# Merging the split products of a block-diagonal matmul, and moving one small sum by half a step

## The chip, the cores and the metric

The kernel runs on one core of a Trainium2 chip. The engines are named as the profile names them: PE multiplies matrices (PEld is its loading of the stationary operand), DVE works on vectors, ACT evaluates functions and copies, POOL is a second, slower vector engine, and SP issues DMAs. The metric is the device time of one execution in microseconds (us). The kernel before took 314.25 us as the median of three runs (313.38 to 314.42).

## The reference

The input x has 2048 tokens of 640 values, and there are 32 heads of 20 values. Two attention branches work on the same x, and a gate per token mixes them: `out = g*a + (1-g)*b`.

Branch A, which the change touches, is linear attention with a learned feature map:

```
q, k, v = split(x @ wqkv)
phi(t) = [softmax(t @ w_phi), softmax(-(t @ w_phi))]      per head, 20 + 20 features
kv = sum over tokens of phi(k)^T v ;  z = sum over tokens of phi(k)
a = ( phi(q) kv ) / ( phi(q) z + 1e-6 ) @ wo
```

Branch B is causal softmax attention within four segments of 512 tokens, plus a memory that is carried from segment to segment, and its own output matrix.

## The kernel before

The work runs in stages, each with an order written out by hand for every engine. Each engine executes its own list in order, and semaphores join the lists.

**Weight folds.** `t @ w_phi` is linear, so the kernel multiplies `w_phi` into the key and query parts of `wqkv` once (`emit_foldM`, L186). The folded matrix has five row chunks of 128. For the keys the five folds lie at the very start (L317), between transposes of the weights and of x, with ACT copying each result out of PSUM. For the queries they lie in one run (L348) after the key stage.

**Key stage** (L338, until about 53 us). 16 chunks of 128 tokens are projected on keys and values, exponentiated by ACT, normalised by DVE and POOL. After it come the kv sums (L382) and the query projections with their exponentials (`emit_pq`, L416), until about 89 us.

**Numerator stage** (L663, about 89 to 127 us). There are 16 chunks `ch` of 128 tokens, and for each chunk two halves, one for each sign `sgn` of the feature map: 32 halves in all. In a half,

- PE computes a numerator (`emit_num`, L477) of 128 x 640 values into one of three PSUM tiles in turn, three halves ahead of its use, and beside it one half of a projection for branch B (`emit_next_half`, L637: five products of 320 columns, which ACT copies out of one of two PSUM buffers);
- DVE multiplies the numerator by its per-head factor (`emit_tt`, L529) into a tile `tt`, of which there are two, one per chunk;
- after both halves POOL adds the two signs into `oA` (L691), which SP sends through a transposing DMA.

The factors come in batches of four chunks. While batch n is being worked on, the denominators of batch n+1 are computed: PE puts them in the free columns of the numerators of the second chunk (k = 1); DVE takes a reciprocal and a product (`emit_rr`, L505) after each of the two halves of k = 1; DVE then sums both signs (`emit_dsum`, L510) after the first half of k = 2; at the end of k = 2, after POOL's `oA`, DVE takes the reciprocal of that sum (L694) and POOL makes the factors from it in two steps (`emit_cs`, L519: L522 and L524). The next batch's first `emit_tt` waits for these. There are three such turns.

**Heads over chunks.** A head has 20 features, a chunk of features has 128 rows, and a PSUM bank holds 16 heads (320 columns). So a head at the border of two chunks (heads 6, 12, 19 and 25) gets its sum from two products. `PIECES` (L63) lists the products of one numerator or fold as (chunk of 128 features, bank, first head, end head). In the kernel before each border head is a product of its own, with 20 columns, apart from the heads of the same chunk that are complete in it:

```python
PIECES = [(0, 0, 0, 7), (1, 0, 6, 7), (1, 0, 7, 13), (2, 0, 12, 13), (2, 0, 13, 16),
          (2, 1, 16, 20), (3, 1, 19, 20), (3, 1, 20, 26), (4, 1, 25, 26), (4, 1, 26, 32)]
FIRST, LAST = {0, 5}, {4, 9}
```

`FIRST` are the products that open a sum in their bank. A later product of the bank adds where the sum has already written, and writes where it has not. In the kernel before no product does both.

**Branch B** (L1052, about 127 us to the end) is driven by 16 double steps, each with bursts of scores on PE (L770), exponentials on ACT (L774), masks on POOL (L781) and products with the values (L824), with dense products put between them.

Of the kernel before, what the change touches and what calls it, by code (L numbers as in the profile page):

```python
# [15 lines left out]
def kernel(  # L16
# [43 lines left out]


    TH = [(P * j // DH, (P * j + P - 1) // DH + 1) for j in range(KC)]
    PIECES = [(0, 0, 0, 7), (1, 0, 6, 7), (1, 0, 7, 13), (2, 0, 12, 13), (2, 0, 13, 16),  # L63
              (2, 1, 16, 20), (3, 1, 19, 20), (3, 1, 20, 26), (4, 1, 25, 26), (4, 1, 26, 32)]
    FIRST, LAST = {0, 5}, {4, 9}
    HW = 8

    gS = res.tile([P, NCH], F32, name="gS")
# [31 lines left out]
    for what in "c w1 w3 x0 x1 g v0 v1".split():  # L100
        n = int(what[1:]) if len(what) > 1 else 0
# [74 lines left out]
    def w2tile(name):  # L176
        return aps.tile([P, 2, 512], F32, name=name, tag="w2")
# [8 lines left out]
    def emit_foldM(WT, dst, ic, eng=nc.scalar.copy):  # L186
        ps = w2tile("fold_ps")
        for n, (j, bk, lo, hi) in enumerate(PIECES):
            h0 = TH[j][0]
            nc.tensor.matmul(ps[:, bk, (lo - 16 * bk) * DH:(hi - 16 * bk) * DH],  # L190
                             lhsT=WT[:, j, ic * P:(ic + 1) * P],
                             rhs=Wphi[:, j, lo - h0:hi - h0, :].rearrange("p h d -> p (h d)"),
                             start=(n in FIRST), stop=(n in LAST))
        eng(out=dst[:, ic, :].rearrange("p (b n) -> p b n", b=2), in_=ps[:, :, 0:320])

    def emit_xT(n):
# [120 lines left out]
    for step in "P T0a T2d M0a T1d M2a T4d T3d M1a X0 M4a X1 M3a k0 g k1 v0 v1 r0 r1".split():  # L317
        n = int(step[1:2] or 0)
        if step[0] == "T":
            emit_foldT(wnat_k, WkT, n, {"a": nc.scalar.copy, "d": nc.vector.tensor_copy}[step[2]])  # L320
        elif step[0] == "M":
            emit_foldM(WkT, WkA, n, {"a": nc.scalar.copy, "d": nc.vector.tensor_copy}[step[2]])
        elif step[0] == "X":
            emit_xT(n)
        elif step[0] == "P":
            for j in (0, 2):
                emit_Wphi(j, nc.vector)
        elif step[0] == "k":
            emit_a1_mm(n, pks, WkA, 320)
        elif step[0] == "v":  # L330
            emit_a1_mm(n, pvs, WvA, 321)
        elif step[0] == "r":
            emit_a1(n)
            emit_zmove(n)
        else:
            emit_gw()
# [11 lines left out]
    for n in range(KC):  # L348
        emit_foldM(WkT, WqA, n)
# [127 lines left out]
    def emit_num(ch, sgn):  # L477
        qb, qc = divmod(ch, HB // P)
        t = nps[(2 * ch + sgn) % 3].tile([P, 2, 512], F32, name="num")
        for n, (j, bk, lo, hi) in enumerate(PIECES):  # L480
            h0 = TH[j][0]
            nc.tensor.matmul(t[:, bk, (lo - 16 * bk) * DH:(hi - 16 * bk) * DH],  # L482
                             lhsT=Eqs[qb, j][:, sgn, qc * P:(qc + 1) * P],
                             rhs=kvn[:, sgn, j, lo - h0:hi - h0, :].rearrange("p h e -> p (h e)"),
                             start=(n in FIRST), stop=(n in LAST))
        return t

    def num_view(t):
        return t[:, :, 0:320].rearrange("p b (h e) -> p b h e", e=DH)

    def den_view(t):

        return t[:, :, 320:448].rearrange("p n (s h e) -> p n s h e", s=2, e=2)
# [11 lines left out]
    def emit_rr(rr, uu, t, o, n):  # L505
        k = slice(o, o + n)
        nc.vector.reciprocal(out=rr[:, k], in_=t[:, :, :, :, 1])  # L507
        nc.vector.tensor_tensor(out=uu[:, k], in0=t[:, :, :, :, 0], in1=rr[:, k], op=ALU.mult)

    def emit_dsum(uu, n):  # L510
        dd = a3w.tile([P, NB, H], F32, name="dd", bufs=1)
        nc.vector.scalar_tensor_tensor(out=dd[:, 0:n], in0=uu[:, 0:n, 0, :], scalar=1e-6,
                                       in1=uu[:, 0:n, 1, :], op0=ALU.add, op1=ALU.add)
        return dd

    def rr_tiles():
        return (a3w.tile([P, NB, 2, H], F32, name="rr"), a3w.tile([P, NB, 2, H], F32, name="uu", bufs=1))

    def emit_cs(chs, rr, dd, o=0):  # L519
        n = len(chs)  # L520
        k = slice(o, o + n)
        nc.gpsimd.tensor_tensor(out=dd[:, k], in0=dd[:, k],  # L522
                                in1=gS[:, chs[0]:chs[0] + n, None].to_broadcast([P, n, H]), op=ALU.mult)
        nc.gpsimd.tensor_tensor(out=rr[:, k], in0=rr[:, k],  # L524
                                in1=dd[:, k, None, :].to_broadcast([P, n, 2, H]), op=ALU.mult)
        for i, ch in enumerate(chs):
            cs_of[ch] = rr[:, o + i]

    def emit_tt(tt, sgn, ps, cs):  # L529
        csb = cs[:, sgn].rearrange("p (b h) -> p b h", b=2)[:, :, :, None].to_broadcast([P, 2, 16, DH])  # L530
        nc.vector.tensor_tensor(out=tt[:, sgn].rearrange("p (b h) d -> p b h d", b=2),  # L531
                                in0=ps, in1=csb, op=ALU.mult)
# [74 lines left out]
    def slot(ch):  # L607

        return ch + (ch >= EARLY)
# [15 lines left out]
    def emit_turn(part, sc, dst):  # L625
        c = sc % 4
        nc.sync.dma_start_transpose(out=dst[:, :, c * P:(c + 1) * P],
                                    in_=stages[part][sc % 2].rearrange("p h e -> p (h e)"))
# [8 lines left out]
    def emit_next_half():  # L637
        if halves:
            emit_half(pps, *halves.pop(0), nc.scalar.copy)
# [10 lines left out]
    def emit_num_at(i):  # L650
        if i < len(order):
            ch, sgn = order[i]
            t = nums[ch, sgn] = emit_num(ch, sgn)
            if ch % 4 == 1 and ch < NCH - 4:
                for n in range(2):
                    emit_den(den_view(t)[:, n], ch + 3 + 2 * sgn + n)
# [6 lines left out]
    for ch in range(NCH):  # L663
        bt = next(n for n, chs in enumerate(BATCH) if ch in chs)
        k = ch - BATCH[bt][0]
        ahead = BATCH[bt + 1] if bt < len(BATCH) - 1 else None
        tt = a3w.tile([P, 2, H, DH], F32, name="tt")
        for sgn in range(2):
            t = nums.pop((ch, sgn))
            emit_tt(tt, sgn, num_view(t), cs_of[ch])  # L670
            if ahead and sgn == 0 and k == 1:
                rr_n, uu = rr_tiles()
            if ahead and (k, sgn) in ((1, 0), (1, 1)):
                emit_rr(rr_n, uu, den_view(t), 2 * sgn, 2)
            for _ in range((ch, sgn) not in IDLE):
                emit_next_half()
            emit_num_at(2 * ch + sgn + 3)
            if ch - 1 in KEYS and sgn == 0:
                nc.scalar.activation(out=ek, in_=ek, func=ACT.Exp, scale=-1.0)
            elif ch - 1 in KEYS:  # L680
                nc.scalar.activation(out=phik, in_=key, func=ACT.Relu)
            if (ch, sgn) in EXPS:
                part = EXPS[ch, sgn]
                nc.scalar.activation(out=(phiks[1][:, 0] if part == "k" else phiq_st)[:, :, 0:DH],
                                     in_=stages[part][0][:, :, 0:DH], func=ACT.Exp)
            if (ch, sgn) in TWICE:
                emit_next_half()
            if ahead and k == 2 and sgn == 0:
                dd = emit_dsum(uu, NB)
        oA = a3w.tile([P, D], BF16, name="oA", bufs=4)  # L690
        nc.gpsimd.tensor_tensor(out=oA.rearrange("p (h d) -> p h d", d=DH),  # L691
                                in0=tt[:, 0], in1=tt[:, 1], op=ALU.add)
        if ahead and k == 2:
            nc.vector.reciprocal(out=dd, in_=dd)  # L694
            emit_cs(ahead, rr_n, dd)
        while turns_due:
            part, c = turns_due.pop(0)
            emit_turn(part, c, (kTs if part == "k" else qTs)[c // 4])
        nc.sync.dma_start_transpose(out=oTA[:, slot(ch)], in_=oA)
        if ch - 2 in KEYS:  # L700
            nc.gpsimd.tensor_tensor(out=phik, in0=phik, in1=ek, op=ALU.add)
        if ch in KEYS:
            key = stages["k"][KEYS[ch] % 2][:, :, 0:DH]
            phik = phiks[0][:, KEYS[ch], :, 0:DH]
            ek = a3w.tile([P, H, DH], BF16, name="ek")
            nc.scalar.activation(out=ek, in_=key, func=ACT.Relu, scale=-1.0)
# [5 lines left out]
    with ExitStack() as bctx:  # L712
# [487 lines left out]
        for ps, lo in quarters:  # L1200
            for k5 in range(KC):
                nc.tensor.matmul(ps, lhsT=oT4[:, 2, k5, :], rhs=WoB[:, k5, lo:lo + 160],
                                 start=(k5 == 0), stop=(k5 == KC - 1))
# [36 lines left out]
```

## Time and profile before

| what | us |
|---|---|
| median of three runs | 314.25 |
| the profiled execution: its own time | 314.52 |
| its span, from first to last instruction | 312.8 |
| PE busy | 302.4 |
| ACT busy | 251.9 |
| DVE busy | 230.3 |
| POOL busy | 205.6 |
| the 32 numerators (L482): products | 320 |
| the ten folds (L190): products | 100 |
| start of the numerator stage, start of branch B's scores | 88.97, 126.8 |

The profile shows one execution. Busy times are sums over a whole engine, and a busy PE is not the same as PE being the limit: matmuls are pipelined, so a row's duration is longer than the pace at which products follow each other. What limits a stage has to be read from the chain of work (which event released which), taken stage by stage.

### The profile page before, as it was taken

Reading aid. Unit: us, or ns where it says so; the run is one execution under the profiler, and the core shown is the slowest. Engines: PE = TensorE matmul, PEld = TensorE weight load, DVE = VectorE, ACT = ScalarE, POOL = GpSimd, SP = SyncE. Lnnn points to the kernel's source line nnn. Section 1 sums busy time; section 2 is a strip of 40 time slices with the busy share of each in tenths; the row PEclk is TensorE's granted clock in tenths of the full one; section 3 lists DMA queues with packets and bytes.
Section 4 is the critical chain, followed back from the end, with each engine's and each line's share of the span. In section 5 each row is a group of like instructions: output and inputs, shape, how many; then the busy total and the mean of one; then the engine's idle time right before and its main releaser. Section 6 shows DMA issues by size and latency. Waiting matters only on the chain.

```text
span 312.8 us, 9844 instructions
## 1 busy us (share of the span) xinstructions
PE 302.4 (97%) x4038; PEld 205.3 (66%) x4038; DVE 230.3 (74%) x532; ACT 251.9 (81%) x320; POOL 205.6 (66%) x310
## 2 busy tenths in 40 slices
PE   8999999999999999999999999999999999999995
PEld 7788877855578788465656666666666666544573
DVE  3477997998779997767758588788656746667773
ACT  4677888357956549899999899999998999899953
POOL 8588599103346989965666667688886767756560
PEclk9999999999999999999999999999999999999999
DMA  7989934439217998775331358343855556334142
GB/s 223 202 173 188 234 103 127 130 88 365 76 27 99 129 142 132 153 103 105 37 69 36 69 111 121 57 91 61 110 92 90 53 106 116 82 82 97 40 115 84
DMA packets 97414, 35.33 MB, mean 113 GB/s; under 512 B 85722, under 2 KB 97370, under 8 KB 97370
## 3 DMA queue, kind: packets, MB, share of 16 engines
q1 hardware_dynamic: 96794, 34.06, 56.3%
q10 hardware_dynamic: 576, 0.66, 0.7%
q8 instruction: 31, 0.51, 0.7%
q14 instruction: 13, 0.11, 0.1%
HBM read 6.10 MB, written 2.62 MB: 28 GB/s over the span
## 4 chain that ended last, share of the span: by engine, by line
PE 68%; ACT 21%; DVE 5%; POOL 3%; issue 2%; ACTq 0%; DVEq 0%; POOLq 0%
ACT PT L774 18%; PE proj L1008 10%; PE st_ps L770 9%; PE proj L948 8%; PE pq L421 7%; PE pk L240 7%; PE pv L240 7%; PE nda L824 5%; PE proj L561 3%; DVE tt L531 2%; PE num L482 2%; PE kv_ps L394 2%; DVE rr L507 2%; POOL oA L691 1%; PE warm L316 1%
## 5 line engine op out<-in xcount | busy, mean ns | idle before, releaser
L774 ACT ACTIVATE PT<-st_ps 128x1024 bf16<-128x1024 f32 x160 | 153.9, 1024 | 11.3 <-PE st_ps L770 8.9
L781 POOL TENSOR_SCALAR_AFFINE_SELECT PT<-PT 128x512 bf16<-128x512 bf16 (+1 forms) x130 | 83.8, 663 | 42.7 <-ACT PT L774 42.3
L259 POOL TENSOR_TENSOR EkSn<-Ek,krec 128x1280 bf16<-128x1280 bf16 x15 | 35.1, 2358 | 9.2 <-DVE krec L258 7.3
L824 PEld LDWEIGHTS <-PT 128*128 128x128 bf16 x1040 | 32.9, 96 | 7.8 <-issue 4.5
L1008 PEld LDWEIGHTS <-xTf 128*128 128x128 bf16 x300 | 26.5, 97 | 14.1 <-issue 5.5
L824 PE MATMUL nda<-vB,PT 128*128 128x21 bf16 x1000 | 34.2, 173 | 0.0
L1014 DVE CAST Z<-proj 128x320 bf16<-128x320 f32 x44 | 21.2, 489 | 16.4 <-PE proj L1008 15.3
L428 ACT ACTIVATE Eq<-pq 128x1024 bf16<-128x1024 f32 x20 | 19.4, 1021 | 12.6 <-PE pq L421 12.6
L255 DVE TENSOR_REDUCE ksum<-Ek 128x64 f32<-128x1280 bf16 x16 | 23.6, 1475 | 7.2 <-ACT Ek L251 7.2
L948 PE MATMUL proj<-WkA,oTA 128*128 128x320 bf16 x160 | 28.3, 300 | 0.0
L531 DVE TENSOR_TENSOR tt<-num,rr 128x640 f32<-128x640 f32 x32 | 25.0, 813 | 4.4 <-POOL rr L524 1.7
L770 PE MATMUL st_ps<-Z 32*128 32x512 bf16 (+3 forms) x256 | 25.2, 299 | 3.0 <-ACT PT L774 2.5
L691 POOL TENSOR_TENSOR oA<-tt 128x640 bf16<-128x640 f32 x16 | 24.6, 1546 | 5.2 <-DVE tt L531 5.0
L770 PE MATMUL st_ps<-Eq 32*128 32x384 bf16 (+3 forms) x256 | 25.6, 298 | 1.9 <-ACT PT L774 1.5
L251 ACT ACTIVATE Ek<-pk 128x640 bf16<-128x640 f32 x32 | 20.8, 703 | 8.1 <-PE pk L240 7.0
L240 PEld LDWEIGHTS <-xTf 128*128 128x128 bf16 x200 | 22.6, 113 | 4.7
L421 PE MATMUL pq<-xTf,WqA 128*128 128x512 bf16 x100 | 22.4, 379 | 0.3 <-issue 0.3
L948 PE MATMUL proj<-WvA,oT 128*128 128x320 bf16 x120 | 21.2, 300 | 0.0
L948 PEld LDWEIGHTS <-oTA 128*128 128x128 bf16 x160 | 13.5, 97 | 8.6 <-issue 4.6
L561 PEld LDWEIGHTS <-xTf 128*128 128x128 bf16 x180 | 15.8, 97 | 4.6
L770 PEld LDWEIGHTS <-Z 32*128 32x128 bf16 x256 | 7.5, 91 | 16.2 <-issue 15.0
L482 PEld LDWEIGHTS <-Eq 128*128 128x128 bf16 x320 | 15.9, 96 | 3.3 <-issue 0.7
(194 smaller groups left out, 584.8 us busy)
## 6 DMA issues: line engine op xcount, KB each, us to landing
Z<-EkSn SPq DMA_DIRECT2D x32, 160.0 KB, 2.8
out_dram<-orow SPq DMA_DIRECT2D x8, 160.0 KB, 1.8
out_dram<-oTA SPq DMA_DIRECT2D x6, 160.0 KB, 1.8
WvA<-in_A_wqkv_dram SPq DMA_DIRECT2D x2, 400.0 KB, 5.9
WvB<-in_B_wv_dram SPq DMA_DIRECT2D x1, 800.0 KB, 4.6
WkB<-in_B_wk_dram SPq DMA_DIRECT2D x1, 800.0 KB, 6.4
WqB<-in_B_wq_dram SPq DMA_DIRECT2D x1, 800.0 KB, 8.1
WkA<-in_A_wo_dram SPq DMA_DIRECT2D x1, 800.0 KB, 11.2
```

The source lines that it names most:

```text
L240: nc.tensor.matmul(ps[:, bk, 0:n], lhsT=key_tokens(c, sc), rhs=rhs, start=(c == 0), stop=(c == by_row[-1][0] if sc == 0 and W is WkA else ...
L259: (nc.vector if sc == NCH - 1 else nc.gpsimd).tensor_tensor(out=EkSn[:, sc].rearrange("p s (h f) -> p (s h) f", f=DH), in0=Ek.rearrange("p ...
L421: nc.tensor.matmul(pq[:, half, :], lhsT=WqA[:, c, j * P:(j + 1) * P], rhs=xq[:, 2 * qb + half, c], start=(c == 0), stop=(c == KC - 1))
L531: nc.vector.tensor_tensor(out=tt[:, sgn].rearrange("p (b h) d -> p b h d", b=2), in0=ps, in1=csb, op=ALU.mult)
L561: nc.tensor.matmul(ps, lhsT=xq[:, sc // 4, cc, sc % 4 * P:(sc % 4 + 1) * P], rhs=W[:, cc, half * 320:(half + 1) * 320], start=(cc == 0), s ...
L691: nc.gpsimd.tensor_tensor(out=oA.rearrange("p (h d) -> p h d", d=DH), in0=tt[:, 0], in1=tt[:, 1], op=ALU.add)
L770: nc.tensor.matmul(ps[:, i - i0, o:o + L - c * P], lhsT=kT[32 * i:32 * i + 32, c * P:(c + 1) * P], rhs=qT[32 * i:32 * i + 32, c * P:L], st ...
L774: nc.scalar.activation(out=PT[:, i0:i0 + 2], in_=ps, func=ACT.Exp, scale=SCALE_B)
L781: nc.gpsimd.affine_select(out=v, in_=v, pattern=[[0, n_i], [1, P]], compare_op=ALU.is_ge, fill=0.0, base=0, channel_multiplier=-1)
L824: nc.tensor.matmul(nd[:, j, i], lhsT=block(st, c)[:, i, (j - c) * P:(j - c + 1) * P], rhs=vB[:, c, 4 * st.g + i, :], start=(c == 0), stop= ...
L948: nc.tensor.matmul(ps, lhsT=oT[:, k % KC], rhs=W[:, k % KC, hs], start=(k == 0), stop=(k == n - 1))
L1008: nc.tensor.matmul(ps, lhsT=xq[:, sc // 4, k, sc % 4 * P:(sc % 4 + 1) * P], rhs=W[:, k, half * 320:(half + 1) * 320], start=(k == 0), stop ...
```

## The change

The change has two parts.

First, `PIECES` is cut from ten products to six: each is now everything that one chunk of features gives to one bank. Where a chunk holds the rest of a border head and also new heads, one product now adds in its first 20 columns and writes in the others. Both `emit_num` and `emit_foldM` use the list, so 32 numerators and 10 folds lose four products and four weight loads each, 168 in all. The number of columns computed stays 720 per numerator or fold. (`skip_group_check` concerns only the building of the program.)

Second, `emit_dsum` moves from the end of the first half of k = 2 to the end of its second half. On DVE the order is before: tt(k=2, first), dsum, tt(k=2, second), reciprocal; and after: tt(k=2, first), tt(k=2, second), dsum, reciprocal. Nothing else changes place on any engine.

```diff
-    PIECES = [(0, 0, 0, 7), (1, 0, 6, 7), (1, 0, 7, 13), (2, 0, 12, 13), (2, 0, 13, 16),
-              (2, 1, 16, 20), (3, 1, 19, 20), (3, 1, 20, 26), (4, 1, 25, 26), (4, 1, 26, 32)]
-    FIRST, LAST = {0, 5}, {4, 9}
+    PIECES = [(0, 0, 0, 7), (1, 0, 6, 13), (2, 0, 12, 16), (2, 1, 16, 20), (3, 1, 19, 26), (4, 1, 25, 32)]
+    FIRST, LAST = {0, 3}, {2, 5}
...
@@ emit_foldM and emit_num
-                             start=(n in FIRST), stop=(n in LAST))
+                             start=(n in FIRST), stop=(n in LAST),
+                             skip_group_check=True)
...
-            if ahead and k == 2 and sgn == 0:
+            if ahead and (k, sgn) == (2, 1):
                 dd = emit_dsum(uu, NB)
```

More of the change, by code (lines that the diff above doesn't have):

```diff
@@ L484, in emit_num @@
                              rhs=kvn[:, sgn, j, lo - h0:hi - h0, :].rearrange("p h e -> p (h e)"),
-                             start=(n in FIRST), stop=(n in LAST))
+                             start=(n in FIRST), stop=(n in LAST),
+                             skip_group_check=True)
         return t
```

## The prediction

> **What bounds the kernel now.** I read the chain of work stage by stage, then the timeline of single engines where it changes hands. The start first (columns: start us, us, what):
>
> ```profile
> 3.92 0.55 PE wtp L182 x5
> ...
> 5.24 0.82 PE fold_ps L190 x10
> 6.06 0.53 PE wtp L182 x5
> 6.59 0.64 PE fold_ps L190 x10
> 7.23 0.56 PE wtp L182 x10
> 7.79 0.38 PE fold_ps L190 x10
> ```
>
> From 5.24 us the chain stays on PE through all five key folds and the key stage. Five transposes take 0.53 us until 6.6 us, and ten take 0.56 after: PE runs at half pace at first. The row of the granted clock says 1.00 all the same.
>
> The numerator stage, in the chain again; one turn of a batch, then the last one:
>
> ```profile
> 94.90 0.88 DVE rr L507
> ...
> 96.00 0.81 DVE tt L531
> 96.82 0.20 DVE dd L512
> 97.02 0.75 DVE tt L531
> 97.76 0.07 issue
> 97.83 1.54 POOL oA L691
> 99.37 0.37 POOL dd L522
> ...
> 99.81 0.72 POOL rr L524
> 100.53 1.51 POOL oA L691
> 102.04 0.02 issue
> 102.06 0.82 DVE tt L531
> ...
> 116.00 0.54 PE num L482 x10
> 116.54 0.68 PE proj L561 x5
> 117.22 0.38 PE num L482 x10
> ```
>
> Up to 116 us the loop is DVE (92.15 to 97.8), POOL (to 102.0), DVE again: PE runs ahead and isn't in it, apart from the first three numerators (88.97 to 92.06). From 116 us the chain is PE's: a numerator 0.38 and a half projection 0.68 in turn, 1.06 a half. But DVE and POOL are close behind:
>
> ```profile
> 124.74 3.05 DVE L531 TENSOR_TENSOR tt<-num,rr 128x640 f32<-128x640 f32 x4 [1.25 <-POOL oA L691]
> 125.62 0.54 PE L482 MATMUL num<-kvn,Eq 128*128 128x140 bf16 x10
> ```
>
> The first of these tt ends at 125.50, and frees the PSUM tile of PE's last numerator, which the chain has at 125.73. PE has 0.2 us on them, no more. Branch B behind it (126.9 to 312.8) hangs on this stage alone for its start.
>
> **The change, part by part.**
>
> *Price of a product.* Five products of 320 columns take 0.68 us, 136 ns each; of 512 columns, 216 (ten queries in 2.16); so 0.417 ns a column and 2.6 on top. The 40 denominator products of 14 to 64 columns take 1.02 us, 25.5 each: the floor. Ten pieces of 140, 20, 120, 20, 60, 80, 20, 120, 20 and 120 columns make 61 + 4 x 25.5 + 3 x 52.6 + 27.6 + 36 = 384 ns; the chain shows 0.38. Six of 140, 140, 80, 80, 140 and 140 make 4 x 61 + 2 x 36 = 316. So 0.07 us less for each numerator or fold. A product that adds in some columns and writes in others is in no row. Bounds: 61 ns, the pace of products that only write or only add (the opening and the later ones of a projection are alike), and 78 ns, the two that it replaces. I take 61, since both kinds of column run at it; at 78 all of this part is nothing.
>
> *Key folds.* Five on the chain: 5 x 0.07 = 0.35. In the half-paced stretch two of them save twice that, but what they leave is filled with more half-paced work, so I count them once. ACT's copies of the results must follow: the third starts at 8.21 as its fold ends, the last ends at 10.23, and the key product that needs it runs at 10.58 at the earliest, so they move along. PE's first product on transposed x stands at 15.0; that DMA was issued at 4.72 and the slowest of its kind took 9.4, so it is there at 14.1. Bounds 0 and 0.5.
>
> *Query folds.* 0.35 less on PE, but PE waits behind them until ACT's five copies end at 57.13 (3.08 us from 54.04, the kv sums start at 57.18). Nothing; if the copies were quicker, up to 0.35.
>
> *First three numerators.* The first tt of k = 1 starts at 92.15, 0.09 behind the denominators that follow the third. 3 x 0.07 = 0.21; the third also needs the PSUM of the last query tile, which ACT leaves at 90.95 against 91.10 for PE, so 0.15.
>
> *Moved sum.* Between tt at 96.00 and tt at 96.93 (timeline) lie 0.93 us; two tt without a sum between them come 0.745 apart (1.49 for two). So POOL's oA starts 0.19 sooner, in three turns. The sum now stands right before the reciprocal that reads it; such a pair starts 0.32 apart (87.80 and 88.12 in the first batch), 0.13 more than the 0.19 saved, so the reciprocal ends 0.13 later in its turn. It ended at 98.61, and POOL took up L522 at 99.33, so 0.7 of slack shrinks to 0.4. The two tt behind it, done at 100.02 and followed by 0.55 of idling until the factors come, keep 0.4 too. No DMA or POOL instruction changes place; SP's transposes follow oA and come sooner.
>
> But the sum takes two operands from SBUF, and it now runs as POOL's oA begins. How two such meet is seen in branch B's timeline:
>
> ```profile
> 201.39 0.64 POOL L781 TENSOR_SCALAR_AFFINE_SELECT PT<-PT 128x512 bf16<-128x512 bf16 x1 [1.24 <-ACT PT L774]
> 201.57 1.14 DVE L980 SCALAR_TENSOR_TENSOR Eq<-Z,ek 128x640 bf16<-128x640 bf16 x1
> ...
> 212.60 0.82 DVE L980 SCALAR_TENSOR_TENSOR Eq<-Z,ek 128x640 bf16<-128x640 bf16 x1
> 212.66 1.26 POOL L781 TENSOR_SCALAR_AFFINE_SELECT PT<-PT 128x512 bf16<-128x512 bf16 x1
> ```
>
> Whichever starts second lasts longer, 1.14 for 0.82, 1.26 for 0.64: it waits for the first. Here the sum starts 0.08 before its tt ends and oA 0.08 after, so DVE is first and POOL waits at most 0.28 - 0.16 = 0.12. A turn then gains 0.07 to 0.19; three, 0.21 to 0.57.
>
> The Trainium skill ("SBUF — State Buffer", Who interferes with whom) says that a DVE instruction with two SBUF inputs contends with a POOL instruction that reads SBUF, and that the one issued first blocks the other for its whole length. The two pairs above agree. By it the three turns give the lower end, 0.21; without it 0.57.
>
> *Last ten numerators.* PE could save 10 x 0.07 = 0.7 here, but the last numerator waits for the tt of 124.74, which waits for POOL's oA. So the end goes with DVE and POOL, plus the 0.2 that PE stood behind them. PE idles for the rest. ACT must copy in 1.06 us a half a projection (0.32) and in some halves an exponential (0.74): just full, at most 0.3 late over four halves, and two buffers carry it.
>
> *Sum.* Numerator stage: 0.15 + (0.21 to 0.57) + 0.2 = 0.55 to 0.9, middle 0.7. With the start 0.35: 1.05 (0.55 to 1.4). Branch B starts that much earlier, all its inputs with it. The profiled execution (span 312.8, 1.7 around it, 314.52) would take 313.45; the median of the runs is 0.27 lower, so 313.2.
>
> **The rivals.**
>
> *The order of sum and oA is the other way round (slower).* If oA gets going before the sum, the sum waits for its 1.54 us. Take the turn at 97.4: oA to 99.0, sum to 99.2, reciprocal to 100.1, then the two tt to 101.6, POOL's next oA to 103.1, where the next tt started at 102.06: a loss of 1.05 in each turn, 3.2 in all, less 0.7 from start and first numerators: 316.7. It decides as soon as the sum starts more than 0.16 us later than I have it. For it: the margin is small. Against it: DVE works in order, with nothing between the two, and POOL needs a semaphore.
>
> *The half-paced start lasts longer (slower).* Fewer products keep PE a little less busy there. If the half pace went on to the end of the first key product (7.23 to 10.86), that would cost 3.6: 316.8; it eats the gain from 2.1 us of further half pace on. Against it: the chain leaves PE no gap between 5.24 and 10.86, after the change as before. The Trainium skill ("TensorE: Matmul & The Clock Gate", Part 1) says that the clock is halved until a window of about 3.4 us was busy; one more such window would, as an estimate from that page, cost 1.7, and the time be 314.9.
>
> *Only a part arrives.* The start gives nothing because a transfer or copy was the limit there after all (0.7 left: 313.55), or the added-and-written product costs 78 ns, which leaves the moved sum: 0.2 to 0.57 less, 313.85.
>
> *Hidden.* Branch B begins earlier but its POOL and DVE meet in other orders; one such swap moves 0.3 to 0.6 (the pairs above). POOL idles 42.7 us before L781, so most of it doesn't count; if it eats the gain: 314.25, if several lie on the chain, up to 0.5 above.
>
> *More.* If PE were the limit in the whole stage, 32 x 0.07 + 0.35 = 2.6: 311.65. DVE's 9.3 us busy of 9.9 in each middle batch speaks against it.
>
> **How the numbers follow.** A measurement of this kernel tells about 0.3% from no change, 0.94 us here. My forecast (0.55 to 1.4 less): 0.6, of which some 0.5 lie beyond 0.94. Only a part: 0.2. Hidden: 0.06 within, 0.04 above 0.3%. The sum held back: 0.06; half pace: 0.03. More: 0.01. So faster 0.52, same 0.35, slower 0.13. The range from 312.4 (the best end with 0.4 of spread between runs) to 314.5 leaves out about 0.15; the forecast's own range is 312.7 to 313.7.
>
> **What would show it.** Right: 192 products at L482 and 60 at L190, a numerator at 0.32 in the chain; the key stage starting at 9.15 instead of 9.50; DVE's two tt of k = 2 0.75 apart and POOL's oA 0.1 to 0.2 sooner in each turn, perhaps at 1.66 instead of 1.54; PE idling before late numerators; the first scores of branch B at 125.8 instead of 126.8, and the same 186 us from there. Wrong: a sum at L512 of more than 1 us; a factor step L522 that waits for DVE; transposes still at half pace after 7.5; branch B longer than before by 0.5 or more.

## The result, and the profile after

The changed kernel takes 312.96 us (median of 22 runs, 312.10 to 314.19); the kernel before took 313.96 in the same sessions (22 runs, 313.28 to 314.68). The ratio is 0.997, with a 95% interval of 0.9961 to 0.9979: 1.0 us, or 0.3%, faster, where 313.2 was predicted. The profiled execution has a span of 311.9 and a time of 313.58, against 312.8 and 314.52.

Some executions of either kernel show a mean granted clock of 0.993 and a branch B that is 1.4 to 1.8 us longer than the 186.0 of the others, so single profiles are compared here by stages ahead of branch B, and not by their spans.

The moments that split the span are PE's first key products, the first numerator (the start of the numerator stage, taken from the chain of work) and branch B's first scores (taken from PE's timeline).

| | before | after | difference |
|---|---|---|---|
| first key product (L240, on xP) | 9.34 | 8.35 | -0.99 |
| first key product on the transposed x | 15.01 | 15.00 | -0.01 |
| first numerator | 88.97 | 88.87 | -0.10 |
| first scores of branch B | 126.78 | 125.98 | -0.80 |
| numerator stage, between the last two | 37.81 | 37.11 | -0.70 |
| branch B, to the end | 186.02 | 185.92 | -0.10 |

So the profile puts 0.70 in the numerator stage, as predicted, but only 0.10 ahead of it, where 0.35 was. The chain of work of the changed kernel shows the stage (start us, us, what):

```profile
88.87 0.63 PE num L482 x12
...
90.89 0.47 PE num L482 x6
...
97.45 1.54 POOL oA L692
99.00 0.37 POOL dd L523
99.36 0.07 issue
99.43 0.60 POOL rr L525
100.03 0.09 issue
100.12 1.54 POOL oA L692
...
116.62 0.32 PE num L482 x6
...
118.00 0.76 DVE tt L532
118.76 0.04 issue
118.80 0.48 PE num L482 x6
```

Two numerators now take 0.63 instead of 0.77, and one in a run of PE 0.32 instead of 0.38. In the turn at 97.4, POOL goes through oA, both factor steps and the next oA with only 0.16 of gaps. Near the end PE waits for DVE (118.00), where the chain before ran on PE alone.

The moved sum on DVE, and the oA beside it on POOL (timeline of each engine: start us, us, engine, line, operation, and in brackets the idle time before and what ended it):

```profile
95.83 1.54 DVE L532 TENSOR_TENSOR tt<-num,rr 128x640 f32<-128x640 f32 x2
97.29 0.28 DVE L513 SCALAR_TENSOR_TENSOR dd<-uu 128x128 f32<-128x128 f32 x1
97.61 0.95 DVE L695 RECIPROCAL dd<-dd 128x128 f32<-128x128 f32 x1
...
107.01 0.36 DVE L513 SCALAR_TENSOR_TENSOR dd<-uu 128x128 f32<-128x128 f32 x1
```

```profile
97.45 1.54 POOL L692 TENSOR_TENSOR oA<-tt 128x640 bf16<-128x640 f32 x1 [1.10 <-DVE tt L532]
...
106.94 0.29 POOL L762 COPY Eq<-omgS 128x128 f32<-128x128 f32 x1
107.19 1.59 POOL L692 TENSOR_TENSOR oA<-tt 128x640 bf16<-128x640 f32 x1
...
116.96 1.55 POOL L692 TENSOR_TENSOR oA<-tt 128x640 bf16<-128x640 f32 x1 [1.11 <-DVE tt L532]
```

In the first and third turn the sum overlaps the start of oA by 0.12 and lasts 0.28, as before, and oA takes its usual 1.54 or 1.55. In the second turn the sum starts while POOL still runs a copy for branch B (L762). There the sum lasts 0.36, overlaps oA by 0.18, and oA lasts 1.59. So POOL's oA is held 0 to 0.05, and the sum is longer by 0.08 once.

At the start, PE arrives early and then waits (timeline of PE, changed kernel):

```profile
8.35 1.52 PE L240 MATMUL pk<-WkA,xP 128*128 128x320 bf16 x10
...
11.73 2.90 PE L240 MATMUL pv<-WvA,xP 128*128 128x321 bf16 x20 [0.28 <-DVE WvA L207]
15.00 1.55 PE L240 MATMUL pk<-WkA,xTf 128*128 128x320 bf16 x10 [0.37 <-DMA xTf<-in_A_x_dram]
```

In the chain of the start the transfer of the transposed x stands as the longest piece:

```profile
4.83 10.12 DMA xTf<-in_A_x_dram
```

It lands at 14.95, and PE's product on it starts at 15.00. In the kernel before, nothing stood between: PE's first key product came at 9.34, and the one on the transposed x 5.67 later, at 15.01, without a wait.

### The profile page after: what moved, and what is told of

It is laid out like the page before. It is cut to its first block, busy times and chain, and to the rows that moved or that the text cites. A ratio compares the mean times of both kernels' runs of the same rounds, so it can differ in the third digit from the quotient of the medians.

```text
span 311.9 us, 9504 instructions
## 1 busy us (share of the span) xinstructions
PE 299.7 (96%) x3866; PEld 201.7 (65%) x3870; DVE 230.3 (74%) x532; ACT 251.1 (81%) x320; POOL 205.6 (66%) x310
## 4 chain that ended last, share of the span: by engine, by line
PE 64%; ACT 20%; POOL 5%; DMA 4%; DVE 4%; issue 2%; SPq 0%; ACTq 0%; DVEq 0%; POOLq 0%
ACT PT L775 17%; PE proj L1009 11%; PE st_ps L771 10%; PE proj L949 8%; PE pq L421 7%; PE pk L240 6%; PE pv L240 6%; PE nda L825 5%; DMA xTf<-in_A_x_dram 3%; POOL oA L692 3%; PE proj L562 2%; DVE tt L532 2%; PE kv_ps L394 2%; PE num L482 2%; DVE rr L508 1%
## 5 line engine op out<-in xcount | busy, mean ns | idle before, releaser
L1009 PEld LDWEIGHTS <-xTf 128*128 128x128 bf16 x300 | 26.5, 97 | 14.1 <-issue 5.5
L240 PEld LDWEIGHTS <-xTf 128*128 128x128 bf16 x200 | 22.6, 113 | 5.3 <-DMA xTf<-in_A_x_dram 0.7
L1009 PE MATMUL proj<-WkB,xTf 128*128 128x320 bf16 x110 | 18.0, 300 | 0.0
```

The lines of the kernel that those rows point to most:

```text
L240: nc.tensor.matmul(ps[:, bk, 0:n], lhsT=key_tokens(c, sc), rhs=rhs, start=(c == 0), stop=(c == by_row[-1][0] if sc == 0 and W is WkA else ...
L1009: nc.tensor.matmul(ps, lhsT=xq[:, sc // 4, k, sc % 4 * P:(sc % 4 + 1) * P], rhs=W[:, k, half * 320:(half + 1) * 320], start=(k == 0), stop ...
```

## The experiments

### One part alone

`fold_only` has six products in the folds and ten in the numerators, `num_only` the reverse, `dsum_only` only the moved sum. For the first two the list of before is kept beside the new one, and one of the two functions goes on using it: `emit_num` in `fold_only`, as here, and `emit_foldM` in `num_only`.

```diff
+    PIECES = [(0, 0, 0, 7), (1, 0, 6, 13), (2, 0, 12, 16), (2, 1, 16, 20), (3, 1, 19, 26), (4, 1, 25, 32)]
+    FIRST, LAST = {0, 3}, {2, 5}
+    PIECES10 = [(0, 0, 0, 7), (1, 0, 6, 7), (1, 0, 7, 13), (2, 0, 12, 13), (2, 0, 13, 16),
+                (2, 1, 16, 20), (3, 1, 19, 20), (3, 1, 20, 26), (4, 1, 25, 26), (4, 1, 26, 32)]
+    FIRST10, LAST10 = {0, 5}, {4, 9}
...
-        for n, (j, bk, lo, hi) in enumerate(PIECES):
+        for n, (j, bk, lo, hi) in enumerate(PIECES10):
...
-                             start=(n in FIRST), stop=(n in LAST))
+                             start=(n in FIRST10), stop=(n in LAST10),
```

The edit of `dsum_only` is one line.

```diff
-            if ahead and k == 2 and sgn == 0:
+            if ahead and (k, sgn) == (2, 1):
```

> Only the ten folds use six products; numerators and the sum as before. Theory (the start is walled by the transposed x): PE is through the folds earlier, by 0.35 us or more, but its first key product on transposed x still starts at 15.0, because that transfer lands there; the numerator stage starts 0 to 0.15 us earlier and the time falls by 0 to 0.15. Rival (the folds' gain of 0.35 goes through and the after kernel merely lost it elsewhere): first product on transposed x at 14.65, time 0.35 less.

> Only the 32 numerators use six products; folds and the sum as before. Theory (DVE and POOL set the first three batches, PE the end): the numerator stage takes 37.89 us before; 0.15 less at the first three numerators and about 0.2 less at the end, so 37.5 to 37.6, time 0.3 to 0.4 less. Rival A (PE carries the whole gain, the moved sum is idle): 37.2, time 0.7 less. Rival B (the moved sum carries it all): 37.9, no change.

> Only the sum of the denominators moves; all products as before. Theory: the two tt of the third chunk come 0.75 instead of 0.93 us apart, each turn of a batch gains 0.2 on DVE and POOL; two of the three turns reach PE's last ten numerators, so the numerator stage takes 37.5 and the time falls by 0.4. Rival A (PE carries the whole gain): 37.9, no change. Rival B (the sum carries it all): 37.2, 0.7 less.

Measured, in one session (before 314.15):

| kernel | median us | ratio to before, 95% | numerator stage us |
|---|---|---|---|
| fold_only | 313.31 | 0.9979 (0.9958 to 1.0000) | 37.77 |
| num_only | 313.78 | 0.9980 (0.9964 to 0.9997) | 37.66 |
| dsum_only | 314.26 | 0.9999 (0.9976 to 1.0023) | 37.68 |

The last column holds the surprise: against 37.81 before, the numerators alone bring 0.15 and the sum alone 0.13, but both together 0.70. The numerators were expected at 37.5 to 37.6 and the sum at 37.5, so the sum missed by most. In `fold_only` the first key product on the transposed x waits for the transfer and comes at 14.52, sooner than either 15.0 or 14.65. The times are too coarse for parts of this size: `num_only` gains 0.63 in time (0.1 to 1.1) and only 0.15 in its stage. The timelines tell why. Here are the starts, counted from the first numerator of each kernel, of the first tt of k = 1, of the first tt of the three batches that wait for new factors, of the tt that PE's last numerator waits for, and of branch B's scores:

| | tt, k = 1 | batch 2 | batch 3 | batch 4 | last | scores |
|---|---|---|---|---|---|---|
| before | 3.18 | 11.59 | 21.53 | 31.46 | 35.77 | 37.81 |
| num_only | 3.11 | 11.52 | 21.45 | 31.39 | 35.69 | 37.66 |
| dsum_only | 3.18 | 11.39 | 21.34 | 31.07 | 35.39 | 37.68 |
| after | 3.11 | 11.32 | 21.11 | 30.83 | 35.14 | 37.11 |

In `num_only` the three turns stay at 8.41, 9.93 and 9.94, as before: PE is quicker and waits. What comes through is 0.07 ahead of the first tt and 0.07 behind the last one, in the last numerator. The timeline of PE in `num_only` at the end:

```profile
123.46 0.48 PE L485 MATMUL num<-kvn,Eq 128*128 128x140 bf16 x6
123.78 0.84 PE L565 MATMUL proj<-WvB,xTf 128*128 128x320 bf16 x5
124.79 0.47 PE L485 MATMUL num<-kvn,Eq 128*128 128x140 bf16 x6 [0.17 <-DVE tt L535]
```

PE now idles 0.17 before its last numerator, for DVE's tt. In `dsum_only` it is the other engine. The first turn is 0.20 shorter, the second isn't (9.95), and the third is 0.20 shorter again; the last tt is 0.38 sooner, but the scores only 0.13. The chain of `dsum_only`:

```profile
98.05 0.38 PE num L482 x10
98.44 0.68 PE proj L561 x5
...
105.46 0.43 PE num L482 x10
105.89 0.05 issue
105.94 0.42 POOL Eq L733
...
124.09 0.38 PE num L482 x10
124.47 0.69 PE proj L561 x5
```

Now PE, at 1.06 a half, is the chain from 88.46 to 105.9 and again from 115.3 to 125.2. The trace of `dsum_only` names no wait of PE between 90 and 126 us, so PE's pace is a limit all the way. In between the chain goes over POOL: three small steps for branch B on POOL (from L733) wait for a numerator, and the oA of that turn stands behind them in POOL's queue. But PE is not all of the second turn's missing 0.20. Counted from the first tt of their batch, the three steps start 6.09 us in, against 6.03 in the changed kernel, so 0.06 is PE's. The rest stands in the third step, a copy that meets the moved sum. Here are POOL's copy in `dsum_only`, the sum beside it on DVE, and the copy in the kernel before:

```profile
106.66 0.43 POOL L761 COPY Eq<-omgS 128x128 f32<-128x128 f32 x1
```

```profile
106.66 0.28 DVE L512 SCALAR_TENSOR_TENSOR dd<-uu 128x128 f32<-128x128 f32 x1
```

```profile
107.38 0.29 POOL L761 COPY Eq<-omgS 128x128 f32<-128x128 f32 x1
```

The copy takes 0.29 in each of the thirteen other profiles and 0.43 here, where it starts together with the sum. It is 0.14 longer, as if the sum had held it.

So the stage had two limits close together: 37.66 with the old loop of DVE and POOL and a quick PE, 37.68 with the old pace of PE and a quicker loop. Each part of the change moves one of them; only both move the end.

The chain of the kernel before already shows PE at work in the second turn:

```profile
106.05 0.54 PE num L482 x10
106.60 0.68 PE proj L561 x5
...
108.34 0.40 PE num L482 x10
```

### Folds and numerators, without the moved sum

`pieces_only` is the changed kernel with the sum left where it was.

```diff
-            if ahead and (k, sgn) == (2, 1):
+            if ahead and k == 2 and sgn == 0:
```

> Folds and numerators use six products, the sum stays where it was. Theory: numerator stage as with the numerators alone, 37.5 to 37.6; start walled as with the folds alone; time 0.3 to 0.5 less. Rival A (PE carries everything): 37.2 and 0.35 from the folds, 1.0 less, as the whole change.

Measured: 313.38 us, ratio 0.9978 (0.9958 to 0.9998), numerator stage 37.66. The folds add nothing to the stage over `num_only`, to the hundredth. The stage is a little above the 37.5 to 37.6 expected, and the time is 0.7 less, where 0.3 to 0.5 less was expected. The remaining 0.55 of the stage comes with the sum, once PE is quick enough.

### The whole change and the folds again

Both kernels as they were, in another session (before 314.30).

> The changed kernel once more, beside the next three. Time 0.9 to 1.1 us less than before; numerator stage (first numerator in the chain to branch B's first scores) 37.1 as in its first profile, against 37.8 before. The start to that stage may differ by 0.7 between executions, since the other profiles show the first key product on transposed x between 14.2 and 15.0.

> The folds alone once more, since the timed runs gave 0.7 less with an interval from 0 to 1.3. Theory (PE and the transfer of transposed x land within 0.5 of each other, and the later one counts): 0.1 to 0.35 less. Rival (the folds carry most of the whole change): 0.7 or more less.

Measured: the whole change 312.93, ratio 0.9955 (0.9934 to 0.9975), stage 37.11 again (as in `after_g` below, and 37.12 in `after_v`; the five kernels with ten-product numerators and the sum in its old place have 37.77 to 37.96); the folds alone 313.71, ratio 0.9989 (0.9974 to 1.0004). So the folds were worth 0.66 us in one session and 0.35 in the other, with 0.5 to 0.7 either way; and `pieces_only` against `num_only` makes it 0.06 by the ratios and 0.40 by the medians. The times don't settle the size of the folds.

The profiles of the start say more. Over the twelve with nearly the same start (those of `after_g` and `before_g` below, and of `flip` and `flip2`, among them), PE's first key product comes at 8.26 to 8.83 in the eight with six-product folds (mean 8.52), and at 8.57 to 9.34 in the four with ten (mean 8.82): 0.30 sooner, where 5 x 0.07 = 0.35 was worked out. The two groups overlap, so this is a mean of few. Of it, 0.04 is left at the first product on the transposed x (means 14.52 and 14.56, between 14.03 and 15.01). In seven of the twelve, the kernel before among them, the one follows the other by 5.67, which is what PE needs by itself. In the other five it comes 0.28 to 0.98 later than that, and PE waits; in four of these the trace names the transfer, in the fifth (`flip2`) an exponential on ACT. Here is PE in `after_again`:

```profile
8.26 1.52 PE L240 MATMUL pk<-WkA,xP 128*128 128x320 bf16 x10
...
14.38 1.55 PE L240 MATMUL pk<-WkA,xTf 128*128 128x320 bf16 x10 [0.28 <-DMA xTf<-in_A_x_dram]
```

One of the four has the ten-product folds of before (`dsum_only`: 8.57, 14.52): the transfer can end the start with either.

### Sending the transfer earlier

SP issues the loads of the gate weights and of WvA just ahead of the transposed x. Issuing the first of them from ACT's queue was meant to bring the transfer forward.

```diff
-            nc.sync.dma_start(out=gw5, in_=gate_w.rearrange("(c p) -> c p", p=P))
+            nc.scalar.dma_start(out=gw5, in_=gate_w.rearrange("(c p) -> c p", p=P))
```

> The changed kernel, with the small load of the gate weights issued from ACT's queue instead of SP's, so that the transposing transfers of x are issued 0.4 us earlier. Theory (PE waits for that transfer after the change): first key product on transposed x 0.1 to 0.4 sooner than 14.9, no wait for the transfer, time 0.1 to 0.4 less than the changed kernel. Rival (the landing hangs on the traffic, not on the issue, or PE never waits): same as the changed kernel.

> The kernel before, with the same load moved to ACT's queue. Theory: with ten products in a fold PE mostly comes last, so 0 to 0.15 less than before. Rival (the transfer was the limit before the change already): as much as it gives the changed kernel, 0.3 to 0.4.

Measured: `after_g` (the edit on the changed kernel) 313.03, ratio 0.9961 (0.9944 to 0.9978); `before_g` (on the kernel before) 314.49, ratio 1.0008 (0.9992 to 1.0024). The edit didn't do what it was to do: SP came to the transposed x at 4.74, against 4.83, since the WvA load ahead of it still started at 3.69. Nothing follows for the transfer. The second attempt moved the WvA loads themselves.

```diff
-            nc.sync.dma_start(out=WvA[:, :, n, 0:320], in_=wsrc(2 * D)[:, :, n * 320:(n + 1) * 320])
+            nc.scalar.dma_start(out=WvA[:, :, n, 0:320], in_=wsrc(2 * D)[:, :, n * 320:(n + 1) * 320])
```

> The changed kernel with the two loads of WvA issued from ACT's queue instead of SP's. This time SP really should come to the transposed x sooner: the two WvA loads took its queue from 3.72 to 4.68 us and the transposed load was issued at 4.83. If the landing of transposed x is what walls the start (theory), the transfer is issued near 3.8, lands by 13 to 14 us, PE's first key product on it no longer waits for the DMA and starts as its value products end, at 14.2 to 14.4 us; the first numerator comes 0.3 to 0.6 earlier than in the changed kernel's first profile (88.87), and the time is 312.6 to 312.9. If the landing doesn't depend on the issue (rival: the transfer is slow because of what else is on its queues), it lands at 14 to 15 us again, PE waits for it, and the time is that of the changed kernel, 312.95. ACT's two more DMA issues may put off its first copy (4.49 us) by up to 0.2. The numerator stage is 37.1 in either case.

> The kernel before with the same two loads issued from ACT's queue. PE is the limit of its start as it stands (no wait for the transfer at 15.01), so the earlier transfer should give nothing here: first key product on transposed x at 14.4 to 15.0, numerator stage 37.8 to 38.0, time 313.9 to 314.2. Against after_v that makes 1.05 to 1.4 for the whole change if the folds count once the transfer is out of the way (0.35 at the start and 0.70 in the numerator stage), and 0.7 to 0.9 if they don't.

Measured: `after_v` 315.52, ratio 1.0052 (1.0028 to 1.0076); `before_v` 316.46, ratio 1.0082 (1.0053 to 1.0112). Both expectations missed. The loads waited on ACT's queue for an earlier transfer (ACT's table load moved from 2.22 to 4.76), so the first fold starts at 6.90 and 6.79 instead of 5.24, and SP gained only 0.3. But the delay gives by accident what was wanted: a start in which PE waits for no transfer at all. The chain of `before_v`, and of `after_v` below it:

```profile
7.34 0.37 PE wtp L182 x5
7.72 0.64 PE fold_ps L190 x10
8.36 1.07 PE wtp L182 x10
...
10.07 0.53 PE xtp L199 x5
10.60 0.52 PE fold_ps L190 x10
11.12 0.28 PE xtp L199 x5
```

```profile
7.39 0.28 PE wtp L181 x5
7.67 0.32 PE fold_ps L189 x6
```

There the first key product on the transposed x comes at 17.29 and 15.68, 1.61 sooner. 0.35 of it would be the five folds, by their price; the rest is half pace, which in this execution of `before_v` lasted until about 10.9 (five transposes 0.53, then 0.28), and in this one of `after_v` was over by 7.4. Here the granted clock shows it: in `before_v`, after PE had idled for 2.07 us ahead of the first fold, it reads 0.50 from 7.5 to 10.5, and in `after_v`, after 1.81 us of idling, 1.00 all through. When it ends varies from run to run: `after_v` itself spread from 313.75 to 316.96. So the 1.61 is not the price of the products. And 0.7 of it was lost again, since the first numerators stand at 90.69 and 89.78. The loss comes behind the last query fold's copy, where PE goes on at 59.46 and 57.83, still 1.63 apart. Between 55 and 65 us PE idles 0.18 and 0.92; of the 0.92, 0.55 is one gap inside the kv sums of `after_v` (60.18 to 60.73), for which the trace names no releaser. Its cause stays open. The numerator stage is 37.79 and 37.12.

### Does the order of the sum and oA matter?

The slower rival was that oA starts first and the sum has to wait for it. `flip` puts an instruction that nobody needs (a fill of a free tile) on DVE ahead of the sum, so that the sum comes when oA is under way; `flip2` a reciprocal of 128 x 32 values in its place.

```diff
+                nc.vector.memset(zt, 0.0)
                 dd = emit_dsum(uu, NB)
```

```diff
+                nc.vector.reciprocal(out=zt.rearrange("p c t -> p (c t)")[:, 0:64].bitcast(F32), in_=uu[:, 0, 0, :])
                 dd = emit_dsum(uu, NB)
```

> The changed kernel with a fill of an idle tile (128x320 words, an estimate of 0.3 to 0.4 us from fills of that kind) put on DVE between the second tt of the third chunk and the sum, so that POOL's addition is under way when the sum starts. Theory (whoever starts second waits for the first): the sum lasts 1.2 to 1.5 us instead of 0.28 in all three turns, the factors come 0.8 to 1.1 later in each, numerator stage 39.5 to 40.4 against 37.1, time 2.4 to 3.3 more than the changed kernel. Rival (the two do not meet, since the sum's part that reads is short): the sum lasts 0.28, the fill alone costs 0.1 to 0.2 a turn, stage 37.4 to 37.8.

> The changed kernel with a reciprocal of 128 x 32 values, read from the SBUF, put on DVE right before the moved sum, in place of the fill of flip; its result is not used. It should start as the tt before it ends and last 0.2 to 0.4 us, so the sum comes when POOL's oA is under way. If a sum with two operands from the SBUF is held by a POOL addition that reads there (the rival of the prediction), the sum ends with oA: 1.2 to 1.5 us, and the numerator stage is 39 to 40 us. If it isn't held (what flip showed), it lasts 0.2 to 0.3 and the stage stays at 37.1 to 37.4, or 37.8 if the reciprocal holds POOL as the fill did (oA 1.8 instead of 1.54).

Measured: `flip` 313.52, ratio 0.9989 (0.9973 to 1.0004), stage 37.82; `flip2` has one execution, 313.48, stage 37.58. DVE and POOL in `flip2`:

```profile
96.70 0.34 DVE L690 RECIPROCAL zt<-uu 128x32 f32<-128x32 f32 x1
96.96 0.23 DVE L513 SCALAR_TENSOR_TENSOR dd<-uu 128x128 f32<-128x128 f32 x1
```

```profile
96.86 1.72 POOL L693 TENSOR_TENSOR oA<-tt 128x640 bf16<-128x640 f32 x1 [1.11 <-DVE tt L532]
...
106.78 1.71 POOL L693 TENSOR_TENSOR oA<-tt 128x640 bf16<-128x640 f32 x1
...
116.66 1.72 POOL L693 TENSOR_TENSOR oA<-tt 128x640 bf16<-128x640 f32 x1 [1.12 <-DVE tt L532]
```

And in `flip`:

```profile
96.34 0.33 DVE L690 MEMSET zt<- 128x320 uint32 x1
96.58 0.23 DVE L513 SCALAR_TENSOR_TENSOR dd<-uu 128x128 f32<-128x128 f32 x1
```

```profile
96.41 1.80 POOL L693 TENSOR_TENSOR oA<-tt 128x640 bf16<-128x640 f32 x1 [1.11 <-DVE tt L532]
...
106.41 1.78 POOL L693 TENSOR_TENSOR oA<-tt 128x640 bf16<-128x640 f32 x1
```

The theory of `flip` missed: the stage is nowhere near 39.5, and the sum lasts 0.23 in both kernels, with oA's row running all beside it. But this doesn't show that a sum which comes second goes free. oA ends 1.54 after the end of the reciprocal (97.04 to 98.58) or the fill (96.67 to 98.21), as if it had started only there. That is 0.18 and 0.26 more than 1.54. If it did start there, the sum, whose rows begin at 96.96 and 96.58, was not second after all, and the order that the rival needs was not brought about.

Nor do these runs show whether it is the fill and the reciprocal that hold oA, or the sum behind them. oA ends 1.39 to 1.40 after the end of the sum in all six turns here, and 1.40 to 1.43 after it in all three turns of the changed kernel (four profiles) and in the first and third of `dsum_only`, which have no fill. So one reading fits them all: POOL's instruction gets going 0.11 to 0.15 before the sum's row ends, and then takes its own time.

The longer copy in `dsum_only` fits as well: the sum ends at 106.94, and a copy of 0.29 that gets going 0.14 before ends at 107.09, as it does. With the two changed about, the 0.36 of the sum in the changed kernel's second turn fits too: POOL's copy ends at 107.23, and 0.28 from 107.09 on gives 107.37. The prediction's own pairs have the same 0.14: its POOL instruction of 212.66 ends at 213.92, so its usual 0.64 begins at 213.28, and the DVE row before it ends at 213.42. This is read from the rows; no run was made to test it. By it the slower rival still stands for a sum that truly comes second.

Over the three turns oA is longer than in the changed kernel by 0.18 + 0.12 + 0.17 = 0.47 in `flip2`, and by 0.26 + 0.19 + 0.26 = 0.71 in `flip`; the numerator stage is longer by 0.47 and by 0.71. So POOL's oA in the three turns is on the path one for one, which the prediction rested on.

## Why the prediction was right, and where its terms were wrong

*The total was right, 313.2 against 312.96*, and so was the mechanism of the larger part. The terms were not all.

*Price of a product: right.* 61 ns was taken for a product that adds in some columns and writes in others, and 0.316 for six; the chain shows 0.32.

*Numerator stage: 0.70 predicted as the middle, 0.70 measured, of other addends.* They can be read from the table of starts. The first three numerators brought 0.07, not 0.15: the third stands at 0.47 instead of 0.32 in the chain, held by ACT's exponential that frees its PSUM tile. The prediction had seen that limit, with 0.15 to spare, since it read 91.10 off the chain, where a piece starts as the one before it ends. The row of that numerator in the timeline of before starts at 91.00, right behind ACT's end at 90.95, so nothing was to spare:

```profile
91.00 0.54 PE L482 MATMUL num<-kvn,Eq 128*128 128x140 bf16 x10
```

The three turns brought 0.20, 0.15 and 0.21, together 0.56, the upper end of the 0.21 to 0.57 given. And the credit of 0.2 for PE being behind DVE and POOL was 0.07, the one last numerator: the last tt of before already set the start of PE's last numerator. By its row, that numerator starts 0.88 after the tt's start in the kernel before (124.74 and 125.62), as it does in the changed kernel and in `num_only`, where PE is seen to wait for it; the 0.2 came from the chain's 125.73. The errors of -0.08, +0.17 (against the middle of 0.39) and -0.13 nearly cancel, so the exact middle is luck.

*The hold of POOL by the sum, taken as up to 0.12 a turn: 0 to 0.05 measured on oA.* The Trainium skill ("SBUF — State Buffer", Who interferes with whom) says that a DVE instruction with two SBUF inputs contends with a POOL instruction that reads there, and that the later one is fully blocked. The trace agrees that they contend: beside the moved sum a copy on POOL was 0.14 longer in `dsum_only`. The size differs: a hold to the end of the sum's row would have brought the three turns to 0.21, and they came out at 0.56. The prediction counted the hold to the end of the row, although its own two pairs have it end 0.14 earlier; 0.12 less 0.14 leaves nothing for the first and third turn.

*Parts that need each other: not in the prediction.* Its sum adds the gain of the numerators and that of the moved sum as if each stood by itself. By the single runs they bring 0.15 and 0.13, by the double run 0.70. That the chain was PE's from 116 us, with DVE and POOL close behind, was seen. The sentence that PE runs ahead and isn't in the loop up to 116 us, apart from the first three numerators, is wrong: the chain of before has PE from 106.05 to 108.73, and `dsum_only` shows PE without a wait all the way. For the whole change this did no harm, since the quicker numerators moved PE's limit out of the way. That PE would stop the sum's gain alone was not worked out, nor that POOL's steps for branch B wait for a numerator and meet the sum in the second turn.

*Key folds: the step that failed in the profiled execution is the claim that the transposed x "is there at 14.1".* In the profiled execution it landed at 14.95 and took 10.12, longer than the 9.4 that the prediction took for the slowest. PE had its first key product 0.99 sooner, of which 0.35 would be the products, by their price, and the rest a half pace that ended sooner, but only 0.10 was left at the numerators. So the rival that only a part arrives, since a transfer limits the start, came true in this execution. Over all executions the size stays open between 0.04 and the 0.35 predicted: the timed total of 1.0 less 0.70 leaves 0.3, with 0.3 either way.

*Query folds: nothing, as predicted.* PE's folds take 2.02 us instead of 2.08, and in the chain the kv sums follow ACT's last copy at 57.20, against 57.18 before. (The prediction says that the kv sums start there; PE's timeline of before has the first of them from 55.39 on.)

*Branch B: unchanged, 186.02 and 185.92.* The rivals of a longer half pace (316.8) and of the other order (316.7) didn't come. Of the first, if anything, the opposite did: the half pace ended sooner. As to the second, the sum starts 0.16 to 0.18 before oA in every turn.

## What to carry to other kernels

Where two engines stand within a few tenths of a microsecond of each other, the gains of two edits on them don't add: take the stage as the later of two walls, and work out both walls for each edit alone and for both together. An idle gap that the chain shows ahead of an engine isn't slack to be won until the event that ends it is shown to move; and a wait of a few tenths is read from the instruction's own row, since the chain's start of a piece can be later by 0.1. And what PE saves at the start is worth only as much as the transfers that it meets next allow.

## What was not expected of the hardware

- Where a DVE sum of two SBUF operands and a POOL instruction that reads SBUF meet, the rows of these runs fit a hold that ends 0.11 to 0.15 before the first one's row does. oA, which starts 0.16 behind a sum of 0.28, wasn't longer, while a copy that started with the sum was 0.14 longer.
- With a fill or a reciprocal put ahead of the sum, oA's row is 0.12 to 0.26 longer than in the changed kernel. Whether these hold it themselves, or only put the sum later, was not tested.
- The end of PE's half pace at the start moves between executions: with the same list of instructions up to there, the first key product came at 9.34, 8.57 and 8.57 (`before`, `num_only`, `dsum_only`), while the granted clock reads 1.00 all through the start in each of the twelve profiles with nearly the same start. It isn't blind to every half pace: in the delayed start of `before_v` it reads 0.50 from 7.5 to 10.5.
- The transposing transfer is no fixed cost either. Its first use came between 14.03 and 15.01 us in twelve profiles of nearly the same start.
